# Local maxima by reductions of one SBUF input, a block's maxima at the step's end, GpSimd's chains interleaved, maxima placed by way of DRAM

## The chip, the core and the metric

The kernel runs on one core of a Trainium2 chip. The metric is the device time of one execution in microseconds, as the median of several executions. The core's engines run side by side and meet through semaphores: TensorE (PE in the profile; PEld are its weight loads), VectorE (DVE), ScalarE (ACT), GpSimd (POOL) and SyncE (SP), which here issues nearly all DMAs, in the order of its queue.

## The reference

Two attention layers of their own inputs and weights, both with S = 2048 positions, D = 576, 32 heads of Dh = 18, in float32. Their results are joined along the last axis.

```python
# A: local, dilated: each position sees 8 earlier ones, 2 apart
W, dil = 8, 2
idx = pos[:, None] - (jnp.arange(W) * dil)[None, :]
logits = jnp.einsum("bhsd,bhswd->bhsw", q, kg) * scale       # kg = k gathered by idx
logits = jnp.where(mask, logits, -1e9)                       # mask = idx >= 0
o = jnp.einsum("bhsw,bhswd->bhsd", softmax(logits), vg)
a = o.reshape(B, S, D) @ wo
# B: full
scores = jnp.einsum("bhqd,bhkd->bhqk", q, k) * scale
o = jnp.einsum("bhqk,bhkd->bhqd", softmax(scores), v)
b = o.reshape(B, S, D) @ wo
```

## The kernel before

**Two stages.** First both layers' inputs are projected by matmuls of split operands (a value is held as an upper part `hi` in fp32r and the rest `lo`). Q and K of B go to DRAM (`dqk`), as do all of A's (`da`). Then come 512 steps of B's attention: 8 groups `g` of 4 heads, 4 blocks `b` of 512 queries each (32 blocks), 16 tiles of 128 keys (`kt`).

**One step.** Four `score` matmuls (line 302) make the scores of 128 keys by 512 queries, one for each head, each in a PSUM bank. ScalarE takes the exponential (line 306) into `e`. `weigh` (line 770) multiplies the `e` of the step before by V and adds into the one bank `po`. Beside these, two and a part maxima are made for a later block: matmuls at line 178, each bank reduced by VectorE (lines 194, 196, 208) into `mx`. Some steps also hold matmuls of an output projection (line 1094, tiles `y`). The order is written by hand: `PLAIN = "D1A30E2B"` names the order of scores (digits) and maxima (letters) in a step. Seven banks are shared out, four for scores and three for everything else.

**Where a block's maxima go.** The softmax needs each query's greatest score before the exponential, so it is subtracted inside the score matmul: rows 54 and 55 of `qs` hold its negative as an upper and a lower part, against rows of ones in `ks`. When the last reduction of a block has been recorded, `least` (line 217) makes the negative maxima `m`; `turn` transposes them (line 224) a step later; `halve` splits them on GpSimd (lines 113, 114) a step after that; `place` issues eight small DMAs on SP (line 235) five steps later, two in the last group. `place` also puts the DMAs on the list `seen`; from four steps later on the first `weigh` matmul of a step is made to wait for the pair of DMAs at the head of that list.

**Local attention.** A's 2048 positions are 8 tiles `j` of 256. Each is spread over 55 steps by `local(j)`, a list of pieces with the step at which each is put on its engine's queue (`agenda`, carried out by `due()` at the end of a step). On GpSimd `match` multiplies q with the shifted keys (line 909) and adds up (line 913), nine times, and makes the logits `lg` (line 916). VectorE takes the maximum over the window of 8 in three halvings `am` (line 928). GpSimd subtracts it (`lower`, line 934), ScalarE takes the exponentials (line 938), GpSimd sums them (`total`), VectorE inverts the sums, and GpSimd multiplies (`share`) and weighs the values in nine rounds (`weighted`: lines 954 to 957). `upper` and `rest` (lines 961, 966) split the result a tile later, `put` stores it to DRAM (`dao`), and `get` (lines 980, 982) loads it back as `at` and `ahl` for the output projection. `get` puts its six loads on `seen` too. A step at which y's matmuls run is at least 7 steps behind its `get`.

**The end of a block.** `finish` copies `po` to `o` (line 781) and normalises it over the next 26 steps: DMAs `den`, `drec`, `rec` (lines 804 to 807), a reciprocal on VectorE (line 805), GpSimd's multiplication and split (lines 808 to 810).

Of the kernel before, what the change touches and what calls it, by code (L numbers as in the profile page):

```python
# [7 lines left out]
F32 = mybir.dt.float32  # L8
# [34 lines left out]

SEEN = 4
# [27 lines left out]
def two_attentions(ctx: ExitStack, tc, xa, wa, woa, xb, wb, wob, out):  # L72
# [32 lines left out]
    do = dram.tile([2, NG - 1, 128, S], F32, name="do")  # L105

# [52 lines left out]
    seen = deque()  # L159

# [7 lines left out]
    def block(g, b):  # L168
# [52 lines left out]
        def turn(m):  # L221

            raw = maxes.tile([128, 32], F32, name="mt", bufs=2)
            nc.vector.transpose(raw, m)
            later(1, lambda: halve(raw))

        def halve(raw):
            mh = maxes.tile([128, 32], F32R, name="mh", bufs=2)
            split_on(nc.gpsimd, mh, raw.bitcast(F32R), raw)
            later(2 if g == NG - 1 else 5, lambda: place(mh, raw))  # L230

        def place(*parts):
            placed.add((g, b))
            for j in range(4):
                seen.append((step + SEEN, [load(ap(qs.bitcast(F32)[54 + k : 128 : 64, b, 0, 32 * j :], (128, 8), (1, 32)),
                                                t.bitcast(F32)[32 * j : 32 * j + 16]) for k, t in enumerate(parts)]))
# [171 lines left out]
    with (tc.tile_pool(name="x", bufs=1, side="right") as xp,  # L408
# [353 lines left out]
        seen = deque((0, d) for _, d in list(seen)[4:])  # L762
# [4 lines left out]
    def weigh(*steps):  # L767
        for g, b, kt, es in steps:
            for i in range(4):
                ins = nc.tensor.matmul(po[32 * i : 32 * i + 19], vs[g][:, kt, 19 * i : 19 * i + 19], es[i],  # L770
                                       start=kt == 0, stop=kt == NT - 1)
# [114 lines left out]
    def local(j):  # L886
# [20 lines left out]
        def match(c):  # L907
            pr = wide()
            nc.gpsimd.tensor_mul(pr, ap(st["q"][:, 2 * c], (SUB, 2), (0, W), (1, SUB)), window(st["k"], c))  # L909
            if c == 0:  # L910
                st["pr"] = pr
            else:
                nc.gpsimd.tensor_add(st["pr"], st["pr"], pr)  # L913
            if c == DH // 2 - 1:
                lg = st["lg"] = work.tile([128, W, SUB], F32, name="lg", bufs=1)
                nc.gpsimd.tensor_add(lg, st["pr"][:, 0], st["pr"][:, 1])
                if j == 0:
                    for w in range(1, W):
                        nc.gpsimd.memset(lg[:32, w, : DIL * w], MASKED)

        def over_window(op, name, n, i=0, of=1):

            if n == i == 0:
                st[name] = work.tile([128, W // 2, SUB], F32, name=name, bufs=1)
            t, half = st[name], W >> n + 1
            src = t if n else st["lg"]
            at, m = half // of * i, half // of
            TREE[name].tensor_tensor(t[:, at : at + m], src[:, at : at + m], src[:, half + at : half + at + m], op=op)  # L928

        def most(*args):  # L930
            over_window(ALU.max, "am", *args)
# [8 lines left out]
        def total(*args):  # L940
            over_window(ALU.add, "as", *args)
# [8 lines left out]
        def weighted(c):  # L950
            if c == 0:
                st["o"] = work.tile([128, DH, SUB], F32, name="ao", bufs=1)
            at = wide()
            nc.gpsimd.tensor_mul(at, ap(st["lg"], (0, 2), (SUB, W), (1, SUB)), window(st["v"], c))  # L954
            nc.gpsimd.tensor_add(at[:, :, :4], at[:, :, :4], at[:, :, 4:])  # L955
            nc.gpsimd.tensor_add(at[:, :, :2], at[:, :, :2], at[:, :, 2:4])
            nc.gpsimd.tensor_add(st["o"][:, 2 * c : 2 * c + 2], at[:, :, 0], at[:, :, 1])
# [14 lines left out]
        def get(n):  # L972
            st["x"] = []
            st["n"] = n
            moved = []
            last = work.tile([128, 128], F32R, name="ahl", bufs=1)
            for i in range(2):
                t = work.tile([128, 4, 128], F32R, name=f"at{i}", bufs=1)
                for s in range(2):
                    moved.append(load(t.bitcast(F32)[:, :, SUB * s : SUB * s + SUB],  # L980
                                      dao[j, i, 2 * n + s, :512].rearrange("(c p) n -> p c n", p=128)))
                moved.append(load(last.bitcast(F32)[64 * i : 64 * i + 64].rearrange("p (s n) -> p s n", s=2),
                                  rows(dao[j, i, 2 * n, 512], (SUB, 64), (D * SUB, 2), (1, SUB))))
# [7 lines left out]
        def sums_of_a(h):  # L991
# [3 lines left out]
            if h == 0:  # L995
# [6 lines left out]
        TREE = {"am": nc.vector, "as": nc.gpsimd}  # L1002
        MOST = ((31, 0), (32, 1), (33, 2))
# [280 lines left out]
```

## Time and profile before

| | |
|---|---|
| median of 3 runs | 1622.85 us (1620.96 to 1625.3) |
| profiled execution | 1621.36 us |
| its span, first to last instruction | 1619.6 us |
| PE busy | 1605.4 us (99%), 13360 instructions |
| DVE busy | 1393.6 us (86%), 2342 instructions |
| ACT busy | 1214.2 us (75%), 2421 instructions |
| POOL busy | 972.4 us (60%), 816 instructions |
| mean granted TensorE clock | 0.998 |

How to read the rows that follow. In a timeline a row is: start in us, duration in us, engine, line, operation, what is written and read, count, and in brackets the idle time of the engine before it with what ended it. A row of waits is: who waited, for whom, total us, times, longest us. A row of one tile is: line, operation, tile, count, shortest/median/longest in ns, first and last start in us. A row of windows is: the stretch, its length, busy us of PE, PEld, DVE, ACT and POOL with their counts, the granted clock, DMA share, GB/s. A group of the page is: line, engine, operation, shapes, count, busy us and mean ns, idle time before. Attention steps begin at 415 us.

### The profile page before, as it was taken

To read this page: it belongs to the slowest core of one execution; us is meant where nothing else is said; L and a number is where in the kernel's file an instruction comes from. 1 tells how busy PE (TensorE), PEld (TensorE's weight loads), DVE (VectorE), ACT (ScalarE), POOL (GpSimd) and SP (SyncE) were. 2 spreads that over 40 slices of the span, in tenths; PEclk is the share of its full clock that TensorE was granted. 3 is DMA by queue.
4 is the path that set the end of the run, shared out by engine and by line. 5 is a ranking of instruction groups with operands and counts; after the bars stand their busy time and mean duration, and the time that the engine had idled before them with its cause. 6 is when DMAs were issued, how large, how long until landed. Compare 5 with 4: busy or idle time off the path is not lost.

```text
span 1619.6 us, 35222 instructions
## 1 busy us (share of the span) xinstructions
PE 1605.4 (99%) x13360; PEld 956.4 (59%) x13360; DVE 1393.6 (86%) x2342; ACT 1214.2 (75%) x2421; POOL 972.4 (60%) x816
## 2 busy tenths in 40 slices
PE   9999999999999999999999999999999999999998
PEld 7999889999544443444444444444444444444776
DVE  5199999999899999999998999999999999999532
ACT  7324432111799999999998999999999998998454
POOL 2305742210266997995995995996995996940100
PEclk9999999999999999999999999999999999999999
DMA  8937955432222343154137225323622232234211
GB/s 259 231 119 193 277 168 135 127 103 79 60 56 67 74 112 90 36 129 115 46 69 178 56 68 143 86 61 90 136 59 82 71 83 77 62 119 144 91 38 60
DMA packets 186056, 172.11 MB, mean 106 GB/s; under 512 B 119152, under 2 KB 132976, under 8 KB 184160
## 3 DMA queue, kind: packets, MB, share of 16 engines
q1 hardware_dynamic: 181024, 158.31, 35.7%
q0 software_dynamic: 4032, 10.63, 3.3%
q8 instruction: 107, 1.75, 0.5%
q10 hardware_dynamic: 832, 0.92, 0.2%
q14 instruction: 61, 0.50, 0.1%
HBM read 96.94 MB, written 71.90 MB: 104 GB/s over the span
## 4 chain that ended last, share of the span: by engine, by line
PE 94%; DVE 2%; DMA 2%; POOL 1%; ACT 0%; issue 0%; SPq 0%; POOLq 0%; ACTq 0%; DVEq 0%
PE po L770 30%; PE bank L302 18%; PE bank L178 18%; PE bank L391 16%; PE bank L1094 7%; PE bank L328 5%; DVE mx L194 1%; DMA at<-dao 1%; DVE am L928 0%; DVE mx L208 0%; POOL xlo L439 0%; DMA rec<-drec 0%; DVE mx L196 0%; DMA first<-xb 0%; DMA dqk<-ohi 0%
## 5 line engine op out<-in xcount | busy, mean ns | idle before, releaser
L306 ACT ACTIVATE e<-bank 128x512 f32<-128x512 f32 x2048 | 1048.4, 608 | 67.7 <-PE bank L302 63.3
L178 PE MATMUL bank<-ks,qs 54*128 54x512 f32 (+1 forms) x2502 | 790.4, 383 | 4.4 <-DVE mx L194 2.6
L194 DVE TENSOR_REDUCE mx<-bank 128x1 f32<-128x512 f32 x1024 | 680.8, 684 | 86.6 <-PE bank L178 63.8
L178 PEld LDWEIGHTS bank<-ks,qs 54*128 54x128 f32 x2502 | 399.2, 184 | 439.2 <-DVE mx L208 348.0
L302 PE MATMUL bank<-qs,ks 56*128 56x512 f32 x2048 | 577.1, 427 | 0.0
L770 PE MATMUL po<-e,v 128*19 128x512 f32 x4096 | 539.2, 601 | 2.3 <-DMA at<-dao 2.3
L196 DVE TENSOR_REDUCE mx<-bank 128x2 f32<-128x512 f32 x570 | 373.6, 685 | 36.9 <-PE bank L178 24.9
L302 PEld LDWEIGHTS bank<-qs,ks 56*128 56x128 f32 x2048 | 303.4, 185 | 41.8 <-ACT e L306 34.3
L208 DVE TENSOR_REDUCE mx<-bank 128x2 f32<-128x512 f32 x454 | 309.7, 682 | 0.0
L909 POOL TENSOR_TENSOR pr<-aq,akv 128x1024 f32<-128x1024 f32 x72 | 158.3, 2202 | 15.4 <-DMA akv<-da 12.9
L954 POOL TENSOR_TENSOR pr<-lg,akv 128x1024 f32<-128x1024 f32 x72 | 158.5, 2201 | 0.6
L913 POOL TENSOR_TENSOR pr<-pr 128x1024 f32<-128x1024 f32 x64 | 152.7, 2385 | 5.0
L770 PEld LDWEIGHTS po<-e,v 128*19 128x19 f32 x4096 | 70.7, 97 | 135.0 <-issue 119.9
L719 ACT ACTIVATE ohi<-bank 128x512 f32<-128x512 f32 (+1 forms) x56 | 30.5, 595 | 155.1 <-issue 110.7
L391 PE MATMUL bank<-xhi,ahi 64*128 64x512 f32 (+1 forms) x448 | 116.3, 390 | 0.0
L391 PE MATMUL bank<-xhi,alo 64*128 64x512 f32 (+1 forms) x448 | 111.7, 390 | 0.0
L391 PE MATMUL bank<-xlo,ahi 64*128 64x512 f32 (+1 forms) x448 | 108.3, 391 | 0.2 <-POOL xlo L439 0.2
L955 POOL TENSOR_TENSOR pr<-pr 128x512 f32<-128x512 f32 x72 | 92.5, 1284 | 5.7
L439 POOL TENSOR_TENSOR alo<-raw,ahi 128x512 fp32r<-128x512 f32 (+1 forms) x14 | 17.6, 1258 | 123.0 <-ACT ahi L438 108.3
L531 POOL TENSOR_TENSOR olo<-olo,ohi 128x512 fp32r<-128x512 f32 x36 | 46.2, 1295 | 62.6 <-ACT ohi L530 57.3
L391 PEld LDWEIGHTS bank<-xhi,ahi 64*128 64x128 f32 (+1 forms) x448 | 64.8, 181 | 3.0
L1094 PE MATMUL bank<-wohi,at 64*128 64x288 f32 x512 | 65.1, 299 | 0.0
(199 smaller groups left out, 1902.5 us busy)
## 6 DMA issues: line engine op xcount, KB each, us to landing
do<-n SPq DMA_DIRECT2D x28, 512.0 KB
da<-ohi SPq DMA_DIRECT2D x52, 256.0 KB
akv<-da SPq DMA_DIRECT2D x64, 175.5 KB
out<-y SPq DMA_DIRECT2D x32, 288.0 KB
qs<-dqk SPq DMA_DIRECT2D x30, 288.0 KB
ks<-dqk SPq DMA_DIRECT2D x30, 288.0 KB
at<-dao SPq DMA_DIRECT2D x64, 128.0 KB
rec<-drec SPq DMA_DIRECT2D x29, 256.0 KB
```

What stands on the lines that cost most here:

```text
L178: return nc.tensor.matmul(ps, qs[rows_, b, p, 128 * t : 128 * t + 128], ks[rows_, p, 512 * k + at : 512 * k + at + n], start=True, stop=True)
L194: nc.vector.tensor_reduce(mx[:, r, p, t, k : k + 1], ps, axis=AX.X, op=ALU.max)
L196: nc.vector.tensor_reduce(mx[:, r, p, t, 2 * k - 2 : 2 * k], ps.rearrange("q (h n) -> q h n", h=2), axis=AX.X, op=ALU.max)
L208: nc.vector.tensor_reduce(mx[:, :, p, t, 2 * k - 2 + i], ps.rearrange("q (h n) -> q h n", h=2), axis=AX.X, op=ALU.max)
L302: nc.tensor.matmul(ps, ks[at, p, 128 * kt : 128 * kt + 128], qs[at, b, p], start=True, stop=True)
L306: nc.scalar.activation(e, ps, AF.Exp, scale=SCALE)
L391: nc.tensor.matmul(ps, a, b, start=start, stop=stop)
L770: ins = nc.tensor.matmul(po[32 * i : 32 * i + 19], vs[g][:, kt, 19 * i : 19 * i + 19], es[i], start=kt == 0, stop=kt == NT - 1)
L909: nc.gpsimd.tensor_mul(pr, ap(st["q"][:, 2 * c], (SUB, 2), (0, W), (1, SUB)), window(st["k"], c))
L913: nc.gpsimd.tensor_add(st["pr"], st["pr"], pr)
L954: nc.gpsimd.tensor_mul(at, ap(st["lg"], (0, 2), (SUB, W), (1, SUB)), window(st["v"], c))
L1094: nc.tensor.matmul(ps, a, b, start=start, stop=stop)
```

## The change

Five things are changed.

1. The maximum over the window is taken by four `tensor_reduce`, 64/4 = 16 positions each, at steps 30 to 33 of a tile, in place of three `tensor_tensor` maxima at steps 31 to 33. A reduction reads `lg` with the window as its inner axis, 64 elements apart.
2. `least` is put on the agenda: at the end of the same step in the attention stage, one slot later in the projections.
3. `match` adds a product one round after it has been made, with a third room for products (the tile `aohi`); `weighted` works on two rounds at once, operation by operation, from the second round on, at the step of the pair's first.
4. `halve` writes both parts into one tile; `order` (two steps later) stores them to a DRAM tile `dm`, query by query; `place` (three steps after that, one in the last group) loads each part with one DMA.
5. The list `seen` is gone with the waits it put on `weigh`; each load is waited for by its first reader.

The queues of TensorE and ScalarE hold the same instructions in the same order as before.

```diff
...
         def made(n):
...
             if left == 0:
-                least()
+                later(int(projecting), least)
...
         def turn(m):
 
-            raw = maxes.tile([128, 32], F32, name="mt", bufs=2)
+            parts = maxes.tile([128, 2, 32], F32R, name="mt", bufs=2)
+            raw = parts[:, 1].bitcast(F32)
             nc.vector.transpose(raw, m)
-            later(1, lambda: halve(raw))
-
-        def halve(raw):
-            mh = maxes.tile([128, 32], F32R, name="mh", bufs=2)
-            split_on(nc.gpsimd, mh, raw.bitcast(F32R), raw)
-            later(2 if g == NG - 1 else 5, lambda: place(mh, raw))
-
-        def place(*parts):
+            later(1, lambda: halve(parts, raw))
+
+        def halve(parts, raw):
+            split_on(nc.gpsimd, parts[:, 0], parts[:, 1], raw)
+            later(2, lambda: order(parts))
+
+        def order(parts):
+
+            for k in range(2):
+                load(rows(dm[g, b, k, 0, 0], (32, 4), (128, 32), (1, 32)), parts[:, k].bitcast(F32))
+            later(1 if g == NG - 1 else 3, place)
+
+        def place():
             placed.add((g, b))
-            for j in range(4):
-                seen.append((step + SEEN, [load(ap(qs.bitcast(F32)[54 + k : 128 : 64, b, 0, 32 * j :], (128, 8), (1, 32)),
-                                                t.bitcast(F32)[32 * j : 32 * j + 16]) for k, t in enumerate(parts)]))
+            for k in range(2):
+                load(qs.bitcast(F32)[54 + k : 128 : 64, b].rearrange("r p n -> r (p n)"),
+                     dm[g, b, k, :16].rearrange("(r i) n -> r (i n)", r=2))
...
     def weigh(*steps):
         for g, b, kt, es in steps:
             for i in range(4):
-                ins = nc.tensor.matmul(po[32 * i : 32 * i + 19], vs[g][:, kt, 19 * i : 19 * i + 19], es[i],
-                                       start=kt == 0, stop=kt == NT - 1)
-                if i == 0 and seen and seen[0][0] <= step:
-                    behind_of(ins, *seen.popleft()[1])
+                nc.tensor.matmul(po[32 * i : 32 * i + 19], vs[g][:, kt, 19 * i : 19 * i + 19], es[i],
+                                 start=kt == 0, stop=kt == NT - 1)
...
         def match(c):
-            pr = wide()
-            nc.gpsimd.tensor_mul(pr, ap(st["q"][:, 2 * c], (SUB, 2), (0, W), (1, SUB)), window(st["k"], c))
-            if c == 0:
-                st["pr"] = pr
-            else:
-                nc.gpsimd.tensor_add(st["pr"], st["pr"], pr)
-            if c == DH // 2 - 1:
+            if c < DH // 2:
+                if c % 2 == 0 and c:
+                    room = work.tile([128, DH, SUB], F32, name="aohi", bufs=1)
+                    pr = ap(room, (W * SUB, 2), (SUB, W), (1, SUB))
+                else:
+                    pr = wide()
+                nc.gpsimd.tensor_mul(pr, ap(st["q"][:, 2 * c], (SUB, 2), (0, W), (1, SUB)), window(st["k"], c))
+                st["prs"] = st.get("prs", []) + [pr]
+            if c > 1:
+                nc.gpsimd.tensor_add(st["prs"][0], st["prs"][0], st["prs"][c - 1])
+            if c == DH // 2:
+                st["pr"] = st["prs"][0]
...
-        def over_window(op, name, n, i=0, of=1):
-
-            if n == i == 0:
-                st[name] = work.tile([128, W // 2, SUB], F32, name=name, bufs=1)
-            t, half = st[name], W >> n + 1
-            src = t if n else st["lg"]
-            at, m = half // of * i, half // of
-            TREE[name].tensor_tensor(t[:, at : at + m], src[:, at : at + m], src[:, half + at : half + at + m], op=op)
-
-        def most(*args):
-            over_window(ALU.max, "am", *args)
+        def over_window(op, name, i, of):
+
+            if i == 0:
+                st[name] = work.tile([128, SUB], F32, name=name, bufs=1)
+            at = slice(SUB // of * i, SUB // of * (i + 1))
+            nc.vector.tensor_reduce(st[name][:, at], st["lg"][:, :, at].rearrange("p w n -> p n w"), axis=AX.X, op=op)
+
+        def most(i, of):
+            over_window(ALU.max, "am", i, of)
...
         def weighted(c):
             if c == 0:
                 st["o"] = work.tile([128, DH, SUB], F32, name="ao", bufs=1)
-            at = wide()
-            nc.gpsimd.tensor_mul(at, ap(st["lg"], (0, 2), (SUB, W), (1, SUB)), window(st["v"], c))
-            nc.gpsimd.tensor_add(at[:, :, :4], at[:, :, :4], at[:, :, 4:])
-            nc.gpsimd.tensor_add(at[:, :, :2], at[:, :, :2], at[:, :, 2:4])
-            nc.gpsimd.tensor_add(st["o"][:, 2 * c : 2 * c + 2], at[:, :, 0], at[:, :, 1])
+            both = [(n, wide()) for n in ((c, c + 1) if c else (c,))]
+            for n, at in both:
+                nc.gpsimd.tensor_mul(at, ap(st["lg"], (0, 2), (SUB, W), (1, SUB)), window(st["v"], n))
+            for n, at in both:
+                nc.gpsimd.tensor_add(at[:, :, :4], at[:, :, :4], at[:, :, 4:])
+            for n, at in both:
+                nc.gpsimd.tensor_add(at[:, :, :2], at[:, :, :2], at[:, :, 2:4])
+            for n, at in both:
+                nc.gpsimd.tensor_add(st["o"][:, 2 * n : 2 * n + 2], at[:, :, 0], at[:, :, 1])
...
         def get(n):
...
-            seen.extend((step + 5, moved[i : i + 2]) for i in range(0, 6, 2))
...
-        MOST = ((31, 0), (32, 1), (33, 2))
+        MOST = ((30, 0, 4), (31, 1, 4), (32, 2, 4), (33, 3, 4))
...
+        for c in range(DH // 2 + 1):
+            pieces.append((MATCH + 5 * min(c, DH // 2 - 1) // 2, lambda c=c: match(c)))
         for c in range(DH // 2):
-            pieces.append((MATCH + 5 * c // 2, lambda c=c: match(c)))
-            pieces.append((WEIGHT + 5 * c // 2, lambda c=c: weighted(c)))
+            if c == 0 or c % 2:
+                pieces.append((WEIGHT + 5 * c // 2, lambda c=c: weighted(c)))
```

More of the change, by code (lines that the diff above doesn't have):

```diff
@@ L42 @@
 AHEAD = 7
-SEEN = 4
 AT = 0
@@ L105, in two_attentions @@
     do = dram.tile([2, NG - 1, 128, S], F32, name="do")
+    dm = dram.tile([NG, NB, 2, 32, 128], F32, name="dm")
     po = p_po.tile([128, 512], F32, name="po")
@@ L761, in two_attentions @@
         projecting = False
-        seen = deque((0, d) for _, d in list(seen)[4:])
     work = ctx.enter_context(tc.tile_pool(name="work", bufs=1, reuse_waits="tile"))
@@ L938, in exponents, with total @@
             nc.scalar.activation(st["lg"][:, at], st["lg"][:, at], AF.Exp, scale=SCALE)
-        def total(*args):
-            over_window(ALU.add, "as", *args)
+        def total(n):
+            if n == 0:
+                st["as"] = work.tile([128, W // 2, SUB], F32, name="as", bufs=1)
+            t, half = st["as"], W >> n + 1
+            src = t if n else st["lg"]
+            nc.gpsimd.tensor_add(t[:, :half], src[:, :half], src[:, half : 2 * half])
         def inverses(n):
@@ L979, in get @@
                 for s in range(2):
[L980 to L983, printed above, removed]
+                    load(t.bitcast(F32)[:, :, SUB * s : SUB * s + SUB],
+                         dao[j, i, 2 * n + s, :512].rearrange("(c p) n -> p c n", p=128))
+                load(last.bitcast(F32)[64 * i : 64 * i + 64].rearrange("p (s n) -> p s n", s=2),
+                     rows(dao[j, i, 2 * n, 512], (SUB, 64), (D * SUB, 2), (1, SUB)))
                 st["x"].append([t[:, c] for c in range(4)])
             st["x"].append(last)
-            seen.extend((step + 5, moved[i : i + 2]) for i in range(0, 6, 2))
         def finished(h):
```

3 lines of the change are left out of this document (removed).

## The prediction

> **What bounds the kernel now.** I read the page first, then the timeline of one ordinary step, then the waits of ScalarE around every place where that rhythm breaks.
>
> ```profile
> L306 ACT ACTIVATE e<-bank 128x512 f32<-128x512 f32 x2048 | 1048.4, 608 | 67.7 <-PE bank L302 63.3
> ```
>
> The attention steps are 512, with four exponentials (line 306) each. TensorE is called 99% busy, but the ends of its matmuls are modelled, so the timeline decides:
>
> ```profile
> 1394.97 9.23 ACT L306 ACTIVATE e<-bank 128x512 f32<-128x512 f32 x18
> 1397.13 0.69 DVE L194 TENSOR_REDUCE mx<-bank 128x1 f32<-128x512 f32 x1 [0.16 <-PE bank L178]
> 1398.33 1.51 DVE L194 TENSOR_REDUCE mx<-bank 128x1 f32<-128x512 f32 x2
> 1398.50 0.18 PEld L178 LDWEIGHTS bank<-ks,qs 54*128 54x128 f32 x1 [0.85 <-DVE mx L208]
> ```
>
> Eighteen exponentials run without a gap in 9.23 us, 0.51 us each, so a step is 4 x 0.51 = 2.04 us and ScalarE sets it. VectorE is nearly full: three reductions and 0.16 us of idle time, always at the end of a step, behind its last reduction. TensorE's weight load waits for a bank that VectorE frees. So anything that holds VectorE or TensorE by more than a few tenths of a microsecond shows as a gap of ScalarE. Such gaps are what the change can win. The instruction orders of TensorE and ScalarE are the same in both kernels.
>
> **Part 1: maxima of local attention, one input in SBUF.** Before, three tensor_tensor maxima per tile j (`am`, line 928), each with two SBUF inputs.
>
> ```profile
> L928 DVE TENSOR_TENSOR am<-am x16: 211/278/2102, 507.3 to 1360.2; 128x128 f32<-128x128 f32 x8, 128x64 f32<-128x64 f32 x8
> L928 DVE TENSOR_TENSOR am<-lg x8: 412/416/2377, 504.9 to 1355.2; 128x256 f32<-128x256 f32 x8
> ```
>
> Minimum and median are close, but the longest takes 2.38 us instead of 0.41. What happens there, in the timeline, in ScalarE's waits from 617 to 632 us, and in the windows (the clock is the eighth column):
>
> ```profile
> 618.43 2.66 POOL L966 TENSOR_TENSOR ao<-ao,aohi 128x1152 fp32r<-128x1152 f32 x1
> 618.99 2.38 DVE L928 TENSOR_TENSOR am<-lg 128x256 f32<-128x256 f32 x1
> ACT e L306 <- PE bank L302: 2.8, 3, 1.5
> 622.00:626.00 4.00, 3.87 (x16) 1.16 (x16) 3.38 (x7) 2.17 (x4) 0.47 (x1) 0.58 1.07 304
> ```
>
> The maximum starts inside GpSimd's subtraction and ends 0.3 us after it (618.43 + 2.66 = 621.09): it waits. TensorE then waits for banks, and right behind its pause the clock falls to 0.58. ScalarE loses 2.8 us. Where GpSimd is idle the same maximum is free:
>
> ```profile
> 991.52 0.42 DVE L928 TENSOR_TENSOR am<-lg 128x256 f32<-128x256 f32 x1
> 984.81 14.53 ACT L306 ACTIVATE e<-bank 128x512 f32<-128x512 f32 x28
> ```
>
> ScalarE runs through it (0.52 us per exponential). Two more tiles have the wait, j = 2 (from 740 us) and j = 7 (from 1353 us). ScalarE's waits there, and the ordinary wait for y of a quiet tile, last row:
>
> ```profile
> ACT e L306 <- PE bank L302: 1.3, 3, 0.6
> ACT y L999 <- PE bank L1094: 2.1, 1, 2.1
> ACT e L306 <- PE bank L302: 1.2, 2, 0.9
> 1000.21 0.41 ACT L999 ACTIVATE y<-bank 128x288 f32<-128x288 f32 x1 [0.88 <-PE bank L1094]
> ```
>
> For j = 2 that is 1.3 us, for j = 7 it is 1.2 + (2.1 - 0.9) = 2.4 us. With 2.8 us the waits cost 6.5 us. The other five tiles lose nothing that I count.
>
> In their place stand four tensor_reduce per tile, 128 elements in and 16 out, each at the end of a step. The nearest row is that of `m` (below, last line):
>
> ```profile
> L842 DVE RECIPROCAL den<-rec x4: 203/217/253, 1493.8 to 1610.6; 128x16 f32<-128x16 f32 x2, 128x8 f32<-128x8 f32 x2
> L217 DVE TENSOR_REDUCE m<-mx x32: 252/253/255, 124.8 to 1513.8; 128x16 f32<-128x96 f32 x32
> ```
>
> It reads SBUF alone and never took over 0.255 us, whatever GpSimd did. From 96 elements in 0.253 us to 512 in 0.69 us (L194 above) is 1.05 ns per element, so 128 take about 0.29 us. The 0.42 us maximum at 991.52 cost ScalarE nothing, so 0.29 us at the same place costs nothing. Below nothing it cannot go. The upper end is that the strided reading is slow, a rival below. I take -6.5 us.
>
> **Part 2: a block's maxima at the step's end.** `m` is made 25 times after 415 us. In 14 of them it lies between two reductions of a step; the first and the last that stand alone, and one that already lies at a step's end, each with ScalarE's row:
>
> ```profile
> 642.71 0.25 DVE L217 TENSOR_REDUCE m<-mx 128x16 f32<-128x96 f32 x1
> 645.56 2.62 ACT L306 ACTIVATE e<-bank 128x512 f32<-128x512 f32 x5 [0.20 <-PE bank L302]
> 1464.67 0.25 DVE L217 TENSOR_REDUCE m<-mx 128x16 f32<-128x96 f32 x1
> 1467.53 2.07 ACT L306 ACTIVATE e<-bank 128x512 f32<-128x512 f32 x4 [0.19 <-PE bank L302]
> 461.86 0.25 DVE L217 TENSOR_REDUCE m<-mx 128x16 f32<-128x96 f32 x1
> 458.77 8.75 ACT L306 ACTIVATE e<-bank 128x512 f32<-128x512 f32 x17
> ```
>
> In the middle it costs ScalarE 0.2 us, at the end none (17 exponentials in 8.75 us, 0.51 each). 14 x 0.2 = 2.8 us; a few will meet a reciprocal or a local maximum at the same step's end, so I take -2.5 us. What follows from `m` (transpose, split) is one step later at most in the projections, where nothing waits for it.
>
> **Part 3: the waits on TensorE that go.** `seen` made a `weigh` matmul (line 770) wait for loads before their use. One such wait costs much:
>
> ```profile
> 860.46 1.05 PE L770 MATMUL po<-e,v 128*19 128x512 f32 x8 [2.32 <-DMA at<-dao]
> 862.15 2.06 ACT L306 ACTIVATE e<-bank 128x512 f32<-128x512 f32 x4 [2.55 <-PE bank L302]
> 865.50 4.66 ACT L306 ACTIVATE e<-bank 128x512 f32<-128x512 f32 x9 [1.28 <-PE bank L302]
> 869.61 0.61 PE L1094 MATMUL bank<-wohi,at 64*128 64x288 f32 x4
> ```
>
> The load landed about 860.4, yet its first user is the matmul at 869.61. Without the wait ScalarE keeps 2.55 + 1.28 = 3.8 us (the second gap is again a slow clock). The use then comes 3.8 us earlier, at 865.8, still 5.4 us behind the landing. What is late next is nothing at that place. The waits now stand at the first use: some 16 loads of `at` x 6 semaphores, in steps that TensorE bounds. A wait instruction takes 0.02 us on SP's queue:
>
> ```profile
> L235 SPq EVENT_SEMAPHORE  x55: 17/17/17, 233.3 to 1517.7; - x55
> ```
>
> 96 x 0.02 = 2 us at most, none if they are absorbed; I take 0.5 us. Sum: -3.3 us.
>
> **Part 4: GpSimd interleaved.** Rows of one `weighted`, chained:
>
> ```profile
> 1398.87 1.28 POOL L955 TENSOR_TENSOR pr<-pr 128x512 f32<-128x512 f32 x1
> 1400.23 0.73 POOL L956 TENSOR_TENSOR pr<-pr 128x256 f32<-128x256 f32 x1
> 1401.04 0.46 POOL L957 TENSOR_TENSOR ao<-pr 128x128 f32<-128x128 f32 x1
> 1401.46 2.20 POOL L954 TENSOR_TENSOR pr<-lg,akv 128x1024 f32<-128x1024 f32 x1
> ```
>
> Dependent instructions start 0.08 us behind the one before (1400.23 - 1400.15), independent ones 0.04 us ahead of its end. So each removed dependence saves 0.12 us: 8 x 3 in `weighted` and 8 x 2 in `match`, 4.8 us per tile. GpSimd is not what ScalarE waits for, so this is 0 us directly; it covers Part 1, whose first reduction comes a step earlier than the first maximum did. The second `weighted` of a pair stands up to 2.5 steps earlier on GpSimd's queue, ahead of splits and of the normalising of `o`: those come at most one chain later (2.20 + 1.28 + 0.73 + 0.46 = 4.7 us), and only SP's stores and the maxima wait for them.
>
> **Part 5: maxima through DRAM.** Eight small DMAs per block become four. The first pair stands 3 steps earlier on SP's queue than the eight did (at the same step in the last group) and may wait for GpSimd's split; the second pair waits for the first to land. Queued behind are `den`, `drec`, the loads of `at` and of the next tile, all asked for 7 steps (14 us) or more before their use. What SP waited for so far, split and small DMA (total, times, longest), and the block with least room (29), last split and first use:
>
> ```profile
> SPq L235 <- POOL mt L114: 83.7, 16, 11.1
> SPq L807 <- DMA drec<-den: 22.9, 13, 5.0
> 1429.37 0.26 POOL L114 TENSOR_TENSOR mt<-mt,mh 128x32 fp32r<-128x32 f32 x1
> 1441.92 0.49 PE L302 MATMUL bank<-qs,ks 56*128 56x512 f32 x1
> ```
>
> Two hops, each estimated at 2 to 5 us from SP's longest wait of 5.0, and about 2 us of issuing need 6 to 12 us; there are 1441.92 - 1429.63 = 12.3 us, and GpSimd comes some 5 us earlier by Part 4. A delay of SP by one split, 11.1 us at worst, stays inside the 14 us of the loads behind it, though with little room. I take 0 us; the bad end is one pause, a rival below.
>
> **Sum.** -6.5 - 2.5 - 3.3 = -12.3 us. The profiled execution took 1621.36 us, so 1609.1 us; it lies 1.5 us below the median of the three runs (1622.85), inside their spread. I give 1609.5 us.
>
> **Rivals.** *Strided reading makes it slower.* The Trainium skill, "SBUF — State Buffer", section "Door 1: The DMA port swizzle", says that SBUF has lines of 16 bytes and that an access to a new line pays; it gives no figure, and by it the reductions exceed 0.29 us. The new reductions step by 64 elements, 256 bytes, at every element. Up to 0.42 us is free, by the row at 991.52. Beyond that each of 32 costs its excess, and 12.3 us are eaten at 0.42 + 12.3/32 = 0.80 us. At eight times 1.05 ns per element a reduction takes 0.15 + 128 x 8.4 ns = 1.23 us, and 32 x 0.81 = 26 us make 1635 us. Against it: `den<-rec` above reads 16 elements 128 bytes apart in 0.253 us at most. Slower by this: 0.04; a milder form, four times, 0.69 us and 32 x 0.27 = 8.6 us, 1618 us: 0.05.
>
> *GpSimd late.* The first reduction needs the logits a step earlier. For j = 7 and where that step ends:
>
> ```profile
> 1353.48 1.28 POOL L916 TENSOR_TENSOR lg<-pr 128x512 f32<-128x512 f32 x1
> 1352.59 1.51 DVE L194 TENSOR_REDUCE mx<-bank 128x1 f32<-128x512 f32 x2
> ```
>
> They are ready at 1354.76, and VectorE would get there at about 1353.3: 1.5 us late as it stands, 3.3 us early with Part 4. If interleaving saves nothing, VectorE waits 1.5 us for j = 7, with a slow clock behind it some 3 us: 1612.5 us. Chance 0.08.
>
> *The maxima come late* at block 29 or a load at its first use: one pause like that at 860 us, 3.8 us: 1613.3 us. Chance 0.07.
>
> *The change doesn't do what it says*: VectorE waits for GpSimd as before. Only parts 2 and 3 stay, 5.8 us: 1617 us with the same offset. Against it: `m` above. Chance 0.06.
>
> **How the numbers follow.** The forecast has 0.70. The 8-in-10 range begins at 1605 us: 6.5 + 2.8 + 3.8 = 13.1 us at the good end of the bounds, 1608.3 us, less 3 us for pauses of 0.1 to 0.3 us that I didn't count in the other five tiles and for the spread of the runs. It ends at 1617 us, which takes in the rivals but for the milder and the full stride. A measurement here tells 0.3% (4.9 us) from no change: faster means below 1618. Faster 0.87, within 0.3% 0.09 (the milder stride, 0.05, and some of the cases at 1617 us with a second pause, 0.04), slower 0.04 (the full stride).
>
> **What would show it.** In the profile after, no reduction of `lg` over 0.42 us; ScalarE without gaps near 618, 742 and 1356 us; no wait for `at` at a `weigh`; fewer slow-clock stretches in mid-span; `m` only behind the last reduction of a step. The forecast is wrong if VectorE waits for `lg`, or if the steps with y's matmuls have grown.

## The result and the profile after

The kernel after takes 1610.59 us (median of four runs, 1610.11 to 1611.22) against 1621.9 us for the kernel before beside it (four runs, 1620.51 to 1625.3). The ratio is 0.9931, with a 95% interval of 0.9919 to 0.9943. The profiled execution took 1610.11 us, with a span of 1608.3 us, 11.3 us shorter than before. The forecast was 1609.5 us.

From the page of the kernel after, the engines' busy times and the group of the exponentials:

```profile
PE 1597.4 (99%) x13360; PEld 956.0 (59%) x13360; DVE 1388.4 (86%) x2350; ACT 1213.3 (75%) x2421; POOL 962.0 (60%) x816
L309 ACT ACTIVATE e<-bank 128x512 f32<-128x512 f32 x2048 | 1047.2, 608 | 58.8 <-PE bank L305 51.8
```

ScalarE's exponentials take as long as before (1047.2 us against 1048.4), but the idle time in front of them fell from 67.7 to 58.8 us. VectorE and GpSimd also do a little less. Since the exponentials are unchanged, the two traces can be laid side by side step by step, four exponentials to a step of about 2.04 us. That comparison carries most of what follows.

**The waits of VectorE for GpSimd are gone.** The local maxima as one tile, and the place at 617 us in the timeline of the kernel after, where a maximum took 2.38 us before:

```profile
L931 DVE TENSOR_REDUCE am<-lg x32: 356/374/384, 502.1 to 1348.0; 128x16 f32<-128x128 f32 x32
617.07 2.65 POOL L977 TENSOR_TENSOR ao<-ao,aohi 128x1152 fp32r<-128x1152 f32 x1
618.19 0.38 DVE L931 TENSOR_REDUCE am<-lg 128x16 f32<-128x128 f32 x1
```

The shortest and the longest of 32 reductions lie 0.03 us apart. The one at 618.19 lies wholly inside GpSimd's subtraction and still takes 0.38 us. The steps around 618, 742 and 1356 us, which took 3.08 + 4.02, 2.42 + 2.76 + 2.60 and 2.14 + 2.59 + 2.18 + 6.01 us before, now take 1.91 + 2.21, 2.04 + 2.07 + 2.17 and 2.04 + 2.06 + 2.10 + 4.33 us: 6.9 us less.

**The pause for a load of `at` is gone, and `m` stands at the step's end.** The timeline of ScalarE around 860 us and 636 us, with an `m` in its midst:

```profile
844.73 15.41 ACT L309 ACTIVATE e<-bank 128x512 f32<-128x512 f32 x30
635.89 9.72 ACT L309 ACTIVATE e<-bank 128x512 f32<-128x512 f32 x19
639.36 0.24 DVE L214 TENSOR_REDUCE m<-mx 128x16 f32<-128x96 f32 x1
```

ScalarE runs through both places at 0.51 us per exponential. The two steps of the pause took 4.61 + 3.35 us before and take 2.04 + 2.04 us now, 3.9 us less.

**A new pause stands near the end.** Step 479, the last ahead of block 30, takes 5.75 us where it took 2.03. SP's queue, TensorE, ScalarE and the windows there:

```profile
1453.60 1.23 SPq L232 DMA_DIRECT2D dm<-mt  x2
1463.79 0.93 SPq L990 DMA_DIRECT2D at<-dao  x2
1467.98 1.06 SPq L238 DMA_DIRECT2D qs<-dm  x2
1472.98 0.47 PE L305 MATMUL bank<-qs,ks 56*128 56x512 f32 x1 [3.36 <-DMA qs<-dm]
1473.48 2.06 ACT L309 ACTIVATE e<-bank 128x512 f32<-128x512 f32 x4 [3.68 <-PE bank L175]
1474.00:1478.00 4.00, 4.00 (x24) 1.59 (x24) 2.57 (x5) 3.52 (x8) 0.10 (x1) 0.57 0.45 166
```

The block's maxima were stored to DRAM (`dm<-mt`) at 1453.60, but they were loaded back into `qs` only at 1467.98. Between the two stand the loads of `at`, and SP could not issue the first of them before 1463.79. The scores of block 30 waited 3.36 us for the maxima. Behind that the granted clock was 0.57 over 4 us. The three steps from 479 lost 3.7 + 0.7 + 0.5 us, and the next two, which are longer ones, were 1.3 us shorter: 3.7 us of the gain were given back. Without that the kernel would have gained some 15 us.

### The profile page after: what moved, and what is told of

Read it like the earlier page. It is cut to its first block, busy times and chain, and to the rows that moved or that the text cites. A ratio compares the mean times of both kernels' runs of the same rounds, so it can differ in the third digit from the quotient of the medians.

```text
span 1608.3 us, 34964 instructions
## 1 busy us (share of the span) xinstructions
PE 1597.4 (99%) x13360; PEld 956.0 (59%) x13360; DVE 1388.4 (86%) x2350; ACT 1213.3 (75%) x2421; POOL 962.0 (60%) x816
## 4 chain that ended last, share of the span: by engine, by line
PE 98%; DVE 1%; DMA 0%; SPq 0%; ACT 0%; issue 0%; POOL 0%; ACTq 0%; POOLq 0%; DVEq 0%
PE po L772 31%; PE bank L305 19%; PE bank L175 19%; PE bank L394 17%; PE bank L1104 7%; PE bank L331 5%; DVE mx L191 0%; PE bank L546 0%; DMA qs<-dm 0%; DMA out<-y 0%; DVE mx L193 0%; PE bank L1079 0%; ACT vs L612 0%; DVE rec L843 0%; POOL xlo L442 0%
## 5 line engine op out<-in xcount | busy, mean ns | idle before, releaser
L309 ACT ACTIVATE e<-bank 128x512 f32<-128x512 f32 x2048 | 1047.2, 608 | 58.8 <-PE bank L305 51.8
L394 PE MATMUL bank<-xhi,ahi 64*128 64x512 f32 (+1 forms) x448 | 120.2, 390 | 0.0
L914 POOL TENSOR_TENSOR pr<-aq,akv 128x1024 f32<-128x1024 f32 x40 | 87.9, 2204 | 10.7 <-PE bank L175 9.6
L917 POOL TENSOR_TENSOR pr<-pr,aohi 128x1024 f32<-128x1024 f32 x32 | 76.6, 2393 | 0.6
L917 POOL TENSOR_TENSOR pr<-pr 128x1024 f32<-128x1024 f32 x32 | 76.4, 2388 | 0.0
L112 POOL CAST mt<-mt 128x32 fp32r<-128x32 f32 x32 | 6.8, 213 | 111.1 <-DVE mt L222 111.1
```

Source lines behind the costliest of these rows:

```text
L309: nc.scalar.activation(e, ps, AF.Exp, scale=SCALE)
L394: nc.tensor.matmul(ps, a, b, start=start, stop=stop)
L917: nc.gpsimd.tensor_add(st["prs"][0], st["prs"][0], st["prs"][c - 1])
```

## The experiments

Kernels e1, e2 and e4 edit the kernel before, e3 edits the kernel after, and e5 to e10 edit e3. The kernel before was run beside each set: its median was 1622.26 us beside e1 to e4, 1620.96 beside e5 to e8, and 1622.07 beside e9 and e10. Differences between kernels of different sets are of medians, and have this scatter of some 1 us in them; the ratios give nearly the same differences. The attention steps begin at 414.5 to 416.4 us in the profiles, but at 412.2 us in e8 and at 419.3 us in e10; such a shift is in the time, though it has nothing to do with the steps behind it.

### e1: the reductions alone

```diff
 (kernel before, with part 1 of the change only)
-        MOST = ((31, 0), (32, 1), (33, 2))
+        MOST = ((30, 0, 4), (31, 1, 4), (32, 2, 4), (33, 3, 4))
...
+            nc.vector.tensor_reduce(st[name][:, at], st["lg"][:, :, at].rearrange("p w n -> p n w"), axis=AX.X, op=op)
```

> The kernel before with one part of the change: the four reductions of the local maximum (steps 30 to 33 of a tile) in place of the three two-input maxima; GpSimd's chains, the waits of the weigh matmuls and the place of the block maxima stay. Theory: the waits of VectorE for GpSimd at 619, 742 and 1355 us go (6.5 us of ScalarE's gaps), but GpSimd is not ahead, so that the first reduction of tile 7 waits about 2 us for the logits, and that of tile 1 a few tenths; net 3 to 5 us faster. Rival: the reductions collide with GpSimd as the maxima did, a longest one of 1 us or more, and the time is within 1 us of before.

Measured: 1615.9 us (five runs) against 1622.26, ratio 0.9963 (0.9951 to 0.9975): 6.4 us less. The timeline of e1 at the last tile, and its waits of TensorE:

```profile
1347.72 1.28 POOL L916 TENSOR_TENSOR lg<-pr 128x512 f32<-128x512 f32 x1
1349.03 0.38 DVE L926 TENSOR_REDUCE am<-lg 128x16 f32<-128x128 f32 x1 [1.51 <-POOL lg L916]
PE po L770 <- DMA at<-dao: 2.2, 1, 2.2
```

The 6.4 us are net of a new wait. The first reduction comes a step earlier than the first maximum did, and GpSimd still works chained: VectorE waits 1.51 us for the logits, and two steps there are 1.0 and 0.45 us longer. The pause for `at` is still there, but no slow clock follows it: its two steps take 4.27 + 2.04 us where they took 4.61 + 3.35. So some 1.6 us of what e1 gains come from that place and not from the maxima.

### e2: the early waits for loads taken away

```diff
 (kernel before)
-            seen.extend((step + 5, moved[i : i + 2]) for i in range(0, 6, 2))
```

> The kernel before without the waits that a weigh matmul makes for the six loads of at and ahl; those for the block maxima stay, and each load is waited for by its first reader. Theory: the pause at 860 us and the slow clock behind it go and come nowhere else, 3.8 us faster (3 to 4.5). Rival: the wait only moves to the first reader in a step that TensorE bounds, no gain or 1 to 2 us slower.

Measured: 1622.0 us (eleven runs) against 1622.26, ratio 0.9994 (0.9984 to 1.0005). Nothing was gained, yet the pause is gone in the timeline; in its place VectorE's waits for GpSimd are longer:

```profile
857.82 12.32 ACT L306 ACTIVATE e<-bank 128x512 f32<-128x512 f32 x24
745.24 2.64 POOL L966 TENSOR_TENSOR ao<-ao,aohi 128x1152 fp32r<-128x1152 f32 x1
745.67 2.35 DVE L928 TENSOR_TENSOR am<-am 128x128 f32<-128x128 f32 x1
885.64 0.35 DVE L945 RECIPROCAL as<-as 128x32 f32<-128x32 f32 x1 [1.61 <-POOL as L928]
```

ScalarE runs 24 exponentials through the place of the pause, which saves 3.9 us. But at 885.64, nine steps behind the place of the pause, a reciprocal waits for GpSimd's sums, which no pause covers any more (+1.05 and +0.55 us). And at 745.67 a maximum stands for 2.35 us against GpSimd's subtraction (three steps +0.87, +0.83, +0.71 us). Together that is 4.0 us. The second place lies ahead of the pause, so that its removal cannot be the cause there; whether the other removed waits moved it or chance did, one profile does not tell. Shown is that the removal has no effect on the median, and that in this execution waits of VectorE for GpSimd took up what the pause left.

### e3: the block's maxima placed ahead of the loads of `at`

```diff
 (kernel after)
-            later(2, lambda: order(parts))
+            later(1 if g == NG - 1 else 2, lambda: order(parts))
```

In the last group the stores, and with them the placing loads, are put on SP's queue a step earlier.

> The changed kernel with one number altered: in the last group the stores of the split maxima are issued one step after the split instead of two, so that the loads that place them stand ahead of the last at loads on SP's queue (one step earlier). Theory: the pause of 3.4 us before the scores of block 30 is SP's queue (the loads of at wait for TensorE with the placing behind them); it goes, and with it the slow clock: 3 to 4.5 us faster than the changed kernel, about 1607 us. Rival: two hops by way of DRAM are too long for the last group wherever they stand; then the pause stays, at least 2 us of it.

Measured: 1605.88 us (four runs, 1605.55 to 1606.79) against 1622.26, ratio 0.99 (0.9887 to 0.9913). This is 4.7 us less than the kernel after, and the fastest of the kernels here but for e9, which is level with it. SP's queue and ScalarE in e3 at block 30:

```profile
1453.52 1.39 SPq L232 DMA_DIRECT2D dm<-mt  x2
1460.84 1.14 SPq L238 DMA_DIRECT2D qs<-dm  x2
1463.70 0.92 SPq L990 DMA_DIRECT2D at<-dao  x2
1465.61 6.13 ACT L309 ACTIVATE e<-bank 128x512 f32<-128x512 f32 x12 [0.87 <-PE bank L305]
```

The stores went out at the same time as in the kernel after and the loads of `at` too; only the placing moved ahead of them, from 1467.98 to 1460.84. Step 479 is 3.7 us shorter, and the two behind it 0.7 and 0.5 us. So it was the order on SP's queue, not the duration of two hops through DRAM, that made the maxima late.

### e4: the path through DRAM alone

```diff
 (kernel before, with part 4 of the diff: halve, order, place; the list seen is kept)
+            seen.append((step + SEEN, [load(qs.bitcast(F32)[54 + k : 128 : 64, b].rearrange("r p n -> r (p n)"),
+                                            dm[g, b, k, :16].rearrange("(r i) n -> r (i n)", r=2)) for k in range(2)]))
```

> The kernel before with one part of the change: the block maxima placed by way of DRAM (stores two steps after the split, loads three steps after that, one in the last group), with the waits of the weigh matmuls kept, now for two loads of a block. Theory: nothing changes until block 30, whose placing stands behind the loads of at on SP's queue; TensorE waits there 2 to 4 us, and with the slow clock the kernel is 2 to 5 us slower than before. Rival: SP's queue has 4 us less to issue per block, loads come earlier, and the pause at 860 us shrinks: 1 to 3 us faster.

Measured: 1622.1 us (twelve runs) against 1622.26, ratio 1.0005 (0.9995 to 1.0015). The waits of TensorE in e4:

```profile
PE bank L308 <- DMA qs<-dm: 3.4, 1, 3.4
PE po L776 <- DMA qs<-dm: 3.4, 2, 2.8
579.71 2.07 ACT L312 ACTIVATE e<-bank 128x512 f32<-128x512 f32 x4 [4.00 <-PE bank L308]
```

The first row is the pause of the kernel after at block 30, here again (step 479, +3.7 us). The second is new: the kept list makes a `weigh` matmul at 577 us wait for maxima that are first used at 762 us, in block 10, and ScalarE loses 4.0 us. Against these, the one profiled execution lacks the pause for `at` (3.9 us) and 4.6 us of the waits for GpSimd near 618 and 742 us. The total is level. Which of the missing waits are due to the edit and which to the chance of one execution, one profile cannot tell.

### e5: two inputs back

```diff
 (e3, with over_window and MOST of the kernel before)
-        MOST = ((30, 0, 4), (31, 1, 4), (32, 2, 4), (33, 3, 4))
+        MOST = ((31, 0), (32, 1), (33, 2))
```

> The kernel of e3 with the three two-input maxima back in place of the four reductions; everything else as in e3. Theory: VectorE waits for GpSimd again wherever the two meet, single maxima of 1 to 2.5 us, 3 to 9 us slower than e3, and the runs spread wider (over 2 us between them, where e3's spread was 1.2 us). Rival: with GpSimd ahead of the steps the maxima find it idle, within 1 us of e3.

Measured: 1608.11 us against 1620.96, ratio 0.9915 (0.9901 to 0.993); e3's was 0.99. The reductions are worth 2.2 us here (1608.11 - 1605.88), a third of their 6.4 us in e1 and less than the 3 to 9 us that were expected; the two intervals overlap, so the size is rough. The runs spread over 1.8 us. The tile `am` of e5:

```profile
L933 DVE TENSOR_TENSOR am<-am x16: 209/250/944, 506.1 to 1350.1; 128x128 f32<-128x128 f32 x8, 128x64 f32<-128x64 f32 x8
L933 DVE TENSOR_TENSOR am<-lg x8: 414/416/1439, 504.0 to 1344.7; 128x256 f32<-128x256 f32 x8
```

The longest maxima take 0.94 and 1.44 us where they took 2.10 and 2.38. The instructions are those of the kernel before; GpSimd and VectorE only meet at other moments. The gaps are again near 618, 742 and 1345 us, but smaller.

### e6: `m` in the middle of a step

```diff
 (e3)
-                later(int(projecting), least)
+                least()
```

> The kernel of e3 with a block's maxima m made where the block's last reduction falls, in mid-step, as before the change. Theory: 14 gaps of ScalarE of 0.2 us come back, 2.5 to 2.8 us slower than e3. Rival: GpSimd and the later steps take the gaps up, under 1 us.

Measured: 1609.47 us (1609.0 to 1609.94) against 1620.96, ratio 0.9922 (0.9908 to 0.9937). That is 3.6 us more than e3. An `m` in e6 and the exponentials behind it:

```profile
1089.78 0.25 DVE L214 TENSOR_REDUCE m<-mx 128x16 f32<-128x96 f32 x1
1092.64 2.64 ACT L309 ACTIVATE e<-bank 128x512 f32<-128x512 f32 x5 [0.18 <-PE bank L305]
```

In e3 there are 19 exponentials in a row at this place. Fourteen such gaps lengthen their steps by 0.21 to 0.32 us each, 3.3 us together: about `m`'s own 0.25 us each, and not only the 0.2 us that ScalarE's row shows.

### e7: GpSimd chained

```diff
 (e3, with match, weighted and their pieces of the kernel before)
-            both = [(n, wide()) for n in ((c, c + 1) if c else (c,))]
+            at = wide()
```

> The kernel of e3 with GpSimd's products and sums chained one behind the other, as before the change. Theory: GpSimd lags behind the faster steps, and VectorE waits for it at the first reduction of tiles 1 and 7 and at the reciprocals of the sums (e2 showed one such wait of 1.6 us): 2 to 5 us slower than e3. Rival: GpSimd's work is off the path, within 0.5 us of e3.

Measured: 1609.31 us (1609.09 to 1609.48) against 1620.96, ratio 0.9921 (0.9907 to 0.9935). That is 3.4 us more than e3. In e7, the last tile's logits and first reduction, and a reciprocal of tile 3; then the logits and the first reduction of the kernel after:

```profile
1344.04 1.27 POOL L916 TENSOR_TENSOR lg<-pr 128x512 f32<-128x512 f32 x1
1345.35 0.38 DVE L926 TENSOR_REDUCE am<-lg 128x16 f32<-128x128 f32 x1 [1.99 <-POOL lg L916]
875.92 0.35 DVE L947 RECIPROCAL as<-as 128x32 f32<-128x32 f32 x1 [1.15 <-POOL as L943]
```

```profile
1338.87 1.28 POOL L921 TENSOR_TENSOR lg<-pr 128x512 f32<-128x512 f32 x1
1341.69 0.38 DVE L931 TENSOR_REDUCE am<-lg 128x16 f32<-128x128 f32 x1
```

Chained, VectorE waits 1.99 us for the logits. Interleaved, they are there 1.54 us before they are read (1341.69 - 1338.87 - 1.28). Together that is 3.5 us, which is about what interleaving gains GpSimd up to that point. The waits for logits and reciprocal cost ScalarE 1.5 + 0.57 and 0.57 + 0.56 us, 3.2 of the 3.4 us.

### e8: a second reduction beside each

```diff
 (e3)
+            spare = maxes.tile([128, SUB // of], F32, name="spare", bufs=2)
+            nc.vector.tensor_reduce(spare, st["lg"][:, 2 * i : 2 * i + 2].rearrange("p a (n w) -> p (n a) w", w=W), axis=AX.X, op=op)
```

The added reductions have the same 128 elements in and 16 out, but read them side by side; nobody reads the result.

> The kernel of e3 with a second reduction of the same size behind each of the 32 reductions of the local maximum, reading unit steps and writing to a tile that nobody reads. Theory: the 0.37 us of the strided reduction against an estimate of 0.29 us is the stride, so the added ones take 0.27 to 0.30 us; both together overrun the idle time at a step's end, 0.1 to 0.3 us for each of 32, 3 to 9 us slower than e3. Rival: 0.37 us is the cost of a reduction of this size, the added ones take as long.

Measured: 1608.34 us against 1620.96, ratio 0.9914 (0.9898 to 0.993), 2.5 us more than e3. Tiles `am` and `spare` of e8, and a step behind a pair:

```profile
L931 DVE TENSOR_REDUCE am<-lg x32: 358/372/384, 499.6 to 1350.3; 128x16 f32<-128x128 f32 x32
L933 DVE TENSOR_REDUCE spare<-lg x32: 266/276/286, 499.9 to 1350.6; 128x16 f32<-128x128 f32 x32
985.31 2.06 ACT L309 ACTIVATE e<-bank 128x512 f32<-128x512 f32 x4 [0.20 <-PE bank L305]
```

Steps of 256 bytes between the elements cost 0.10 us of 0.372. A further 0.276 us of VectorE at the end of the same step opens a gap of 0.20 us. So a single strided reduction is covered, but hardly more is: 0.65 us (0.372 + 0.276) is too much by 0.2 us. The 2.5 us between the medians don't show the whole price. In the profile the attention steps together take 5.8 us longer than in e3, which is 0.18 us for each of the 32 pairs, as expected; but the attention begins 2.3 us earlier (412.2 us against 414.5), and the runs don't tell why.

### e9: the early waits for the loads of `at` put back

```diff
 (e3)
+            seen.extend((step + 5, moved[i : i + 2]) for i in range(0, 6, 2))
...
+                if i == 0 and seen and seen[0][0] <= step:
+                    behind_of(ins, *seen.popleft()[1])
```

> The kernel of e3 with the waits back that a weigh matmul made for the six loads of at and ahl (two loads each, from five steps behind their issue on); the block maxima stay without such waits. Theory: the pause that before showed at 860 us comes back, with its slow clock 2 to 4 us slower than e3; in e1 2.2 us of it were left, so it depends on how far ahead of the steps SP's loads are. Rival: with the faster queue the loads have landed by then, within 0.5 us of e3.

Measured: 1605.84 us (1605.26 to 1606.05) against 1622.07, ratio 0.99 (0.9885 to 0.9915): e3's time. SP's queue and ScalarE in e9 near 840 us; then the `ahl` load of the same tile in the kernel before:

```profile
839.27 1.15 SPq L995 DMA_DIRECT2D at<-dao  x2
846.52 2.86 SPq L997 DMA_DIRECT2D ahl<-dao  x1
837.72 20.39 ACT L311 ACTIVATE e<-bank 128x512 f32<-128x512 f32 x40
```

```profile
856.57 2.83 SPq L982 DMA_DIRECT2D ahl<-dao  x1
```

The load is issued 10 us earlier than before. The steps are earlier too at this place: step 204, that of the pause, begins at 857.5 us before and at 852.0 us in e9. Against it the load is 4.5 us earlier (5.5 us ahead of it instead of 1.0). The loads have landed when the matmul asks for them, and the waits hold nothing up. To cost 3.8 us it took both, the early wait and a late load: in e2, without the wait, the same load is issued 1.1 us ahead of step 204, and no pause follows either.

### e10: the maxima placed directly

```diff
 (e3, with turn, halve and place of the kernel before, without seen)
-            for k in range(2):
-                load(qs.bitcast(F32)[54 + k : 128 : 64, b].rearrange("r p n -> r (p n)"), dm[...])
+            for j in range(4):
+                for k, t in enumerate(parts):
+                    load(ap(qs.bitcast(F32)[54 + k : 128 : 64, b, 0, 32 * j :], (128, 8), (1, 32)), t.bitcast(F32)[32 * j : 32 * j + 16])
```

> The kernel of e3 with the block maxima placed by eight small loads straight from SBUF as before the change, five steps after the split (two in the last group), and without waits at weigh. Theory: the way by DRAM is worth nothing by itself, within 0.7 us of e3, since every block but the last few has 20 us and more of room and the first score waits for eight semaphores without a gap. Rival: the eight issues of 0.5 us hold SP's queue and the eight waits hold TensorE in steps that it bounds: 1 to 4 us slower than e3.

Measured: 1610.99 us (six runs, 1610.11 to 1613.2) against 1622.07, ratio 0.9935 (0.9922 to 0.9948). That is 5.1 us more than e3. The timeline of e10 in the projections, the first and the last of the eight placings; what waited behind; and a reciprocal:

```profile
149.53 0.63 SPq L233 DMA_DIRECT2D qs<-mh  x1
159.26 0.50 SPq L233 DMA_DIRECT2D qs<-mt  x1
173.06 0.63 ACT L436 ACTIVATE xhi<-raw 128x512 fp32r<-128x512 f32 x1 [10.55 <-DMA raw<-xa]
175.38 0.51 PE L389 MATMUL bank<-xhi,whi 64*128 64x512 f32 x2 [1.81 <-ACT olo L527]
881.50 0.35 DVE L947 RECIPROCAL as<-as 128x32 f32<-128x32 f32 x1 [2.09 <-POOL as L943]
```

Eight small DMAs occupy SP's queue from 149.5 to 159.8 us. The loads of `raw` behind them come late, ScalarE waits 10.55 us and TensorE 1.81 us. The attention starts at 419.3 us, where e3's starts at 414.5: 4.8 us of the difference. The late reciprocal adds 1.5 + 0.56 us; the profiled execution is the slowest of the six, so the others may lack it. The stall in the projections was seen in one profile; the six runs all lie above e3's, and the difference is larger than both expectations.

But the kernel before has the same eight DMAs at this place. Its last placing there and the same `raw`:

```profile
158.04 0.50 SPq L235 DMA_DIRECT2D qs<-mt  x1
171.17 0.63 ACT L438 ACTIVATE xhi<-raw 128x512 fp32r<-128x512 f32 x1 [6.94 <-DMA raw<-xa]
```

Its `raw` is there 1.9 us earlier than e10's, TensorE doesn't pause, and the attention starts at 415.2 us; with the path through DRAM added (e4) it starts at 415.0. So in the kernel before the eight DMAs cost the projections nothing, and the 5.1 us are their price beside the other changes only. In the attention steps the path through DRAM does bring SP ahead: the last load of `ahl` ahead of step 204 is issued 5.8 us before that step in e3 and 1.3 us before it in e10.

## Why the prediction was right, and where its steps were not

**The sum came out near, partly by errors that cancel.** The forecast was -12.3 us, measured were -11.3 us of span. Three terms gained more than stated, and one that stood at nothing gave 3.7 us back, so part of the hit is luck.

**Part 1 (-6.5 us).** The mechanism holds: no reduction of the kernel after waits for GpSimd, and the three named places gained 6.9 us in the profiled executions. Alone it gave 6.4 us, with 1.6 us of the pause for `at` in it and a new wait for the logits against it. Two details were off. A reduction takes 0.374 us, not the estimated 0.29 us: `m`, from which it was scaled, gives no row for elements 256 bytes apart, and e8 puts 0.10 us on the stride. So the rule about 16-byte lines in the Trainium skill, "SBUF — State Buffer", section "Door 1: The DMA port swizzle", is compatible with this trace (0.372 against 0.276 us), though the factor is 1.35 and not the four or eight of the rival. And the term isn't a property of the instruction: with other moments of meeting (e5) it was 2.2 us. The cover at the step's end was right for 0.37 us and is narrow, as e8 shows; of the steps with reductions only two of one tile grew by more than 0.1 us (374 and 375, by 0.20 and 0.17 us).

**Part 2 (-2.5 us).** Its count of 14 was right, the size was low. Between the kernels before and after, 14 steps got shorter by 0.20 to 0.32 us each, 3.2 us together; between e6 and e3 the medians differ by 3.6 us. The gap of 0.20 us that ScalarE's row shows is not the whole of what an `m` costs.

**Part 3 (-3.3 us).** The pause at 860 us went, 3.9 us. But the step from there to a gain of its own was wrong. With the waits alone removed nothing was gained (e2), and with the waits put back nothing was lost (e9). "What is late next is nothing at that place" held at that place, but in e2 a reciprocal waited for GpSimd nine steps later. The 0.5 us for the waits at the first readers didn't show: of the 30 steps with y's matmuls ahead of step 479, the one that grew most grew by 0.17 us.

**Part 4 (0 us directly).** Right in what it covers: the prediction had VectorE 1.5 us late at the last tile without interleaving and 3.3 us early with it. Measured were 1.51 us late in e1, 1.99 us late in e7 and 1.54 us early after. The gain up to that point is 3.5 us, not 4.8 us; 4.8 us counts the whole tile, which may be the reason. As cover it is worth 3.4 us, and the rival *GpSimd late* had priced that absence at 3 us.

**Part 5 (0 us).** This is the step that failed. The rival *the maxima come late* came true, at its price (3.4 us of waiting, 3.7 us in all, against 3.8), but at block 30 and by another way. The two hops had been measured against block 29's room of 12.3 us. What decided was SP's order: the second pair of DMAs stands a step later in the last group than the eight did, now behind the loads of `at`, and those wait for TensorE. In the waits of SP, before and after, the row was there:

```profile
SPq L980 <- PE bank L302: 16.3, 4, 13.1
```

```profile
SPq L990 <- PE bank L305: 23.5, 2, 14.3
```

Of these waits 2.4 us lie at this place before (1478 us) and 9.2 us after (1464 us); the longest ones lie elsewhere, near 1225 and 1214 us, and hold up nothing. The prediction listed SP's waits for GpSimd and for DMAs and asked what is queued behind the placing. It did not ask what the placing is now queued behind. It also left out SP's queue in the projections. That made no difference here, since the attention starts at 415.2 us before and 414.6 us after, but beside the other changes the eight DMAs would have cost about 5 us (e10).

**The parts don't add.** Taken from e3 one at a time, part 1 is worth 2.2 us, part 2 3.6, part 4 3.4, the waits of part 3 nothing and part 5 5.1 us: 14.3 us of the 16.4 us between the kernel before and e3. Added alone to the kernel before, part 1 gives 6.4 us and part 5 nothing, nor do the waits for `at` taken away; parts 2 and 4 were not added alone.

## What to carry to other kernels

When a transfer is split into two hops on one in-order queue, look for every instruction between the two that waits for something else; the row of that queue's waits names it, and moving the second hop by a single step was worth 4.7 us here. A gap that is removed while two engines still collide may come back at the next place where they meet, so the price of a wait holds only for the setting in which it was read. Work put at the end of a step is free only up to a few tenths of a microsecond, and a second piece at the same place costs most of its own time (in e8, 0.18 us of 0.276).

## What the runs showed of the hardware that was not expected

**The clock falls after some short pauses of TensorE, not after all.** Windows over the 3.4 us that begin 0.7 us after TensorE resumes in the kernel before (near 622 us), the resuming matmul, and the same two rows of e7:

```profile
622.72:626.12 3.40, 3.40 (x16) 0.98 (x16) 2.66 (x6) 2.01 (x4) 0.59 (x1) 0.51 1.09 279
622.02 0.38 PE L178 MATMUL bank<-ks,qs 54*128 54x256 f32 x1 [1.29 <-DVE mx L194]
```

```profile
1346.00:1351.00 5.00, 4.53 (x32) 1.88 (x32) 5.00 (x10) 3.65 (x8) 4.84 (x5) 1.00 0.49 167
1346.38 0.38 PE L175 MATMUL bank<-ks,qs 54*128 54x256 f32 x1 [1.41 <-DVE mx L191]
```

After a pause of 1.29 us the clock was half for 3.4 us; after 1.41 us in e7 it stayed full. The pauses of 1.81 us in e10 and 3.36 us in the kernel after had such a stretch behind them; one of 2.17 us in e1 had none:

```profile
855.84 1.05 PE L770 MATMUL po<-e,v 128*19 128x512 f32 x8 [2.17 <-DMA at<-dao]
853.00:862.00 9.00, 6.83 (x59) 2.93 (x59) 6.46 (x13) 6.79 (x15) 3.72 (x3) 1.00 0.71 164
```

The length of the pause alone doesn't decide it. What the slow stretches between 100 and 1500 us have in common is that each lasts 3.41 us, and that two of one trace start a whole number of 3.413 us apart: 238.94 us in the kernel before (622.67 and 861.61 us), which is 70 times, and 126.29 us in e2 (624.50 and 750.79 us), which is 37 times. That speaks for a clock that changes on a fixed grid, so that it may count where on the grid a pause falls; what exactly decides, the runs don't tell.

**The time spreads more where VectorE and GpSimd meet by chance.** The kernel before ranges over 8.7 us in 23 runs and e4 over 7.6 us in twelve. Both have two-input maxima and a chained GpSimd. The kernel after (1.1 us in four), e3 (1.2 us in four) and e5 (1.8 us) lie closer together, though these have fewer runs. In e5 the two-input maxima are back, and in e7 (0.4 us in five) the chained GpSimd, so neither alone makes the spread. The clock has a part in it: in e4 the slowest run had a mean granted clock of 0.994 and the fastest 0.999. That the meetings are the cause is argued here and not shown.
